# Loading the first two token tiles of x on two DMA queues and starting the first key products between their transposes

## The chip, the cores and the metric

The kernel runs on one core of a Trainium2 chip. The metric is device time in microseconds (us). The kernel before takes 179.36 us, the median of five runs (178.54 to 179.41).

## The reference

Two blocks read the same input x (2048 tokens, 512 features, bf16) and are mixed by a gate per token:

```python
x = A_x
g = _sigmoid((x * gate_w).sum(-1, keepdims=True))
a = _A_ref(x, A_wqkv, A_wo)      # linear attention, 32 heads of 16
b = _B_ref(x, B_w1, B_w3, B_w2)  # silu(x w1) * (x w3), times w2; F = 1376
return g * a + (1 - g) * b
```

In the attention block q, k, v = x wqkv; q and k go through phi(t) = (t + 1 if t > 0 else exp(t)) + 1e-6. Per head, kv is the sum over tokens of phi(k) times v and z the sum of phi(k); the output is phi(q) kv / (phi(q) z + 1e-6), times wo.

## The kernel before, in words

Tokens are cut into 16 tiles of 128, and these into four blocks of 512. All of x and all weights are held in SBUF. x is needed in two layouts: `x_sb` (tokens on partitions) and `xT` (features on partitions, in four chunks `kc` of 128). For tiles 2 to 15, `xT` comes by transposing DMAs from HBM (L87, L91). For tiles 0 and 1 TensorE makes it from `x_sb` (`emit_xT`, L169): four transposes of 128x128 against the identity `ident` per tile. They go into PSUM in two pairs; VectorE copies the pair of chunks 0 and 1 to `xT` (L179), ScalarE the pair of chunks 2 and 3 (L181).

The order of the loads is that of their issue. On the sync queue (SP): x tiles 0 and 1 in one transfer of 256 KB (L82), the second half of wk (chunks 2 and 3, L84), the transposing load of tiles 2 and 3 (L87), then the later blocks of x and the other weights. On ScalarE's queue: the first half of wk (chunks 0 and 1, L83). In the transfer of L82, partition p takes the token rows 2p and 2p + 1, which lie together in HBM (2 KB per partition); tile j then holds every second row, and the output of tiles 0 and 1 is stored back by the same view (`out_first`, L81 and L376). GpSimd (POOL) makes the identity first (L59), and then fills the block mask, the padding of w2r and two buffers `hr` (L117 to L135).

TensorE's order is the order of the code, written out by hand from L150 on. It begins with `emit_warm` (L158): matmuls on constants whose result nobody reads, six of 512 columns and three of 128 (L165). After these come the transposes of tile 0, those of tile 1, and then the key products of the first block, four per tile (one for each chunk), each of 128x512 (`emit_k_mm`, L183). The first six of them are interleaved between tiles 0 and 1:

```python
    emit_xT(0)
    emit_xT(1)
    for kc, t in ((0, 0), (1, 0), (0, 1), (1, 1), (2, 0), (3, 0)):
        emit_k_mm(k0[t], t, kc)
```

A tile's products end in `emit_k_phi` (L189): ScalarE takes exp, VectorE forms phi(k) into `pk_sb`, POOL adds it up in `pks`. From tile 4 on, products of keys alternate with those of XP, the sum over tokens of x times phi(k) (`emit_xp`, L202), from which kv is made later (L436). Then queries, the feed-forward block (`emit_ffn`, L302) and the outputs (`emit_out`, L335) follow block by block on TensorE.

Of the kernel before, what the change touches and what calls it, by code (L numbers as in the profile page):

```python
# [13 lines left out]
BF16 = mybir.dt.bfloat16  # L14
# [3 lines left out]
def kernel(  # L18
# [12 lines left out]
    nc = tc.nc  # L31
    P = nc.NUM_PARTITIONS
# [7 lines left out]
    TB = 512  # L40
# [8 lines left out]
    x2d = A_x.flatten_outer_dims()  # L49
    out2d = out.flatten_outer_dims()  # L50

    consts = ctx.enter_context(tc.tile_pool(name="consts", bufs=1))
# [2 lines left out]
    psM = ctx.enter_context(tc.tile_pool(name="psM", bufs=4, space=bass.MemoryType.PSUM))  # L55


    ident = consts.tile([P, P], BF16, name="ident")
    make_identity(nc, ident[:])  # L59


    x_sb = consts.tile([P, NT, D], BF16, name="x_sb")
    xT = consts.tile([P, KC, S], BF16, name="xT")
    wk_sb = consts.tile([P, KC, D], BF16, name="wk_sb")
# [12 lines left out]
    x_r = x2d.rearrange("(t p) d -> p t d", p=P)  # L77
    dq = nc.sync
    TF = 2
    x_first = x2d[0 : TF * P, :].rearrange("(p j) d -> p j d", j=TF)  # L80
    out_first = out2d[0 : TF * P, :].rearrange("(p j) d -> j p d", j=TF)  # L81
    dq.dma_start(out=x_sb[:, 0:TF, :], in_=x_first)  # L82
    nc.scalar.dma_start(out=wk_sb[:, 0:2, :], in_=wqkv_r[:, 0:2, D : 2 * D])  # L83
    dq.dma_start(out=wk_sb[:, 2:4, :], in_=wqkv_r[:, 2:4, D : 2 * D])  # L84
    pre = consts.tile([1, 1], FP32, name="pre")
    nc.scalar.activation(out=pre[:], in_=nc.const_aps.tensor(0.0, [1, 1], FP32), func=ACT.Exp)
    dq.dma_start(  # L87
        out=xT[:, :, TF * P : TB], in_=x2d[TF * P : TB, :], transpose=True
    )
    for tb in range(1, NTB):  # L90
        dq.dma_start(  # L91
            out=xT[:, :, tb * TB : (tb + 1) * TB], in_=x2d[tb * TB : (tb + 1) * TB, :],
# [7 lines left out]
    with nc.allow_non_contiguous_dma(reason="one gate weight per partition and chunk"):  # L100
        dq.dma_start(
            out=wr_sb[:, :, 2 * FR : NR], in_=gate_w.rearrange("(kc d o) -> d kc o", d=P, o=1)
        )
    dq.dma_start(out=wv_sb[:], in_=wqkv_r[:, :, 2 * D : 3 * D])
    for fsl in (slice(0, FM // 2), slice(FM // 2, FM)):
# [13 lines left out]
        out=bm, in_=bm, pattern=[[-Dh, HPC], [0, Dh]], compare_op=ALU.is_ge, fill=0.0,  # L119
# [3 lines left out]
        out=bm, in_=bm, pattern=[[Dh, HPC], [0, Dh]], compare_op=ALU.is_ge, fill=0.0,  # L123
# [34 lines left out]
    def emit_warm(*widths):  # L158
        warm = psX.tile([P, TB], FP32, tag="XP3", name="warm")
        for n in widths:  # L160
            nc.tensor.matmul(  # L161
                warm[:, 0:n], lhsT=warm_l, rhs=warm_r[:, 0:n], start=True, stop=True
            )

    emit_warm(TB, TB, TB, TB, TB, TB, P, P, P)  # L165

    st = {}

    def emit_xT(t):  # L169
        for h in range(2):  # L170
            xTp = psX.tile([P, 2, P], BF16, tag=f"XP{(2 * t + h) % 4}", name="xTp")
            for j in range(2):
                kc = 2 * h + j
                nc.tensor.transpose(  # L174
                    out=xTp[:, j, :], in_=x_sb[:, t, kc * P : (kc + 1) * P], identity=ident[:]
                )
            xT_t = xT[:, 2 * h : 2 * h + 2, t * P : (t + 1) * P]
            if h == 0:
                nc.vector.tensor_copy(out=xT_t, in_=xTp[:])  # L179
            else:  # L180
                nc.scalar.activation(out=xT_t, in_=xTp[:], func=ACT.Copy)  # L181

    def emit_k_mm(k_ps, t, kc):  # L183
        nc.tensor.matmul(  # L184
            k_ps[:], lhsT=xT[:, kc, t * P : (t + 1) * P], rhs=wk_sb[:, kc, :],
            start=(kc == 0), stop=(kc == KC - 1),
        )
# [148 lines left out]
    def emit_out(tb, tt):  # L336
        t = tb * TPB + tt
        tsl = slice(tt * P, (tt + 1) * P)

        if t < NT - 1:  # L340
            parts = [(0, D, True)]
        else:
            h, q7 = D // 2, 7 * D // 8
            parts = [(0, h, True), (h, q7, True), (q7, D, True)]
        if t < NT - 1:
            o_out = work.tile([P, D], BF16, tag="o_out", name="o_out")
        else:
            o_out = consts.tile([P, D], BF16, name="o_last")
        lo = 0
        for i, (a, b, store) in enumerate(parts):  # L350
            o_ps = psX.tile([P, b - a], FP32, tag=f"XP{2 + (tt + i) % 2}", name="o_ps")
            for c in range(KC):
                nc.tensor.matmul(  # L353
                    o_ps[:], lhsT=st[tb, "pqT"][:, c, tsl], rhs=W_sb[:, c, a:b],
                    start=(c == 0), stop=False,
                )
            nc.tensor.matmul(  # L357
                o_ps[:], lhsT=st[tb, "hTr"][:, tsl], rhs=w2r_sb[:, a:b],
                start=False, stop=False,
            )  # L360
            for fc in range(FC):
                nc.tensor.matmul(  # L362
                    o_ps[:], lhsT=st[tb, "hT"][:, fc, tsl], rhs=w2_sb[:, fc, a:b],
                    start=False, stop=(fc == FC - 1),
                )
            if i < 2:
                nc.scalar.activation(  # L367
                    out=o_out[:, a:b], in_=o_ps[:], func=ACT.Copy, scale=omg[:, t : t + 1]
                )
            else:  # L370
                nc.vector.tensor_scalar(  # L371
                    out=o_out[:, a:b], in0=o_ps[:], scalar1=omg[:, t : t + 1], scalar2=None,
                    op0=ALU.mult,
                )
            if store:
                rows = out_first[t] if t < TF else out2d[t * P : (t + 1) * P, :]  # L376
                eng = nc.scalar if i == 1 else nc.sync
                eng.dma_start(out=rows[:, lo:b], in_=o_out[:, lo:b])
                lo = b


    k0 = [psM.tile([P, D], FP32, tag="mm", name=f"k0_{t}") for t in range(TPB)]
    emit_xT(0)
    emit_xT(1)
    for kc, t in ((0, 0), (1, 0), (0, 1), (1, 1), (2, 0), (3, 0)):
        emit_k_mm(k0[t], t, kc)
    emit_k_phi(k0[0], 0)
    for t in range(1, TPB):
# [15 lines left out]
    with tc.manual_schedule(engines={ENG.DVE}):  # L404
# [18 lines left out]
        for dc in range(KC):  # L423
# [9 lines left out]
            out=z_sb[:].rearrange("p (b f) -> p b f", f=Q),  # L433
            in_=z_col[:, :, None].to_broadcast([P, NB, Q]),
        )
        kvT_ps = psX.tile([P, KC, P], FP32, tag="XP0", name="kvT_ps")  # L436
        for c in range(KC):
# [7 lines left out]
            out=kvT_sb[:], in0=kvT_ps[:],  # L445
# [22 lines left out]
    for tb in range(NTB):  # L468
        for fc in range(FC if tb == 0 else 0, FC):
            emit_ffn(tb, fc)  # L470
        nx = tb + 1
        for tt in range(TPB):
            if nx < NTB:
                emit_q(nx, tt, psX, "XP0")
                if tt % 2 == 0:
                    emit_rem(nx, tt // 2, psX, "XP1")
                    if tt == 2:
                        emit_omg(nx)
            emit_out(tb, tt)
            if nx < NTB:  # L480
                emit_den(nx, tt)
        if nx < NTB:
            emit_norm(nx)
# [30 lines left out]
```

## Time and profile before

| what | value |
|---|---|
| median of 5 runs | 179.36 us (178.54 to 179.41) |
| the five runs | 179.40, 179.33, 178.54, 179.41, 179.36 us |
| profiled execution's own time | 179.52 us |
| its span | 177.7 us |
| TensorE busy | 173.3 us, 98% of the span |
| VectorE busy | 118.7 us, 67% |
| ScalarE busy | 65.5 us, 37% |
| POOL busy | 63.7 us, 36% |
| HBM read, written | 8.42 MB, 2.10 MB |

All times in the profile count from the start of its span. PE is TensorE's matmuls, PEld its weight loads, DVE is VectorE, ACT ScalarE, POOL GpSimd and SP SyncE; "SPq" and "ACTq" are their DMA issues. A row of the timeline has the start, the time covered, engine, line, operation, output and inputs, and the count. A matmul's duration contains the time in the array's pipeline, so that the distance between the starts of two matmuls that follow each other is its cost, not its duration. A row of the windows has the window, its length, the busy time of PE, PEld, DVE, ACT and POOL (with counts), the granted TensorE clock, the mean busy share of the DMA engines, and GB/s. A row of the DMA issues has the line's tile and source, the queue, the count, the size, and the time from issue to landing.

### The profile page before, as it was taken

How to read it: one execution, taken by the hardware profiler on the slowest of the kernel's cores; microseconds unless marked ns; L12 is line 12 of the kernel's file. 1: busy time of each engine (PE TensorE's matmuls, PEld its weight loads, DVE VectorE, ACT ScalarE, POOL GpSimd, SP SyncE). 2: the span in 40 equal slices, each digit the busy share in tenths (PEclk: the TensorE clock that was granted, in tenths of full speed). 3: DMA queues.
4: the chain of work that ended last, by engine and by line, in shares of the span. 5: the costliest groups of instructions: out<-in, count | busy, mean ns of one | idle time of the engine just before them, and what ended most of it. 6: DMA issues, size and time to landing. Idle time of an engine off the chain costs nothing.

```text
span 177.7 us, 2457 instructions
## 1 busy us (share of the span) xinstructions
PE 173.3 (98%) x867; PEld 84.1 (47%) x883; DVE 118.7 (67%) x204; ACT 65.5 (37%) x123; POOL 63.7 (36%) x80
## 2 busy tenths in 40 slices
PE   8999999999999999999999999999999999999993
PEld 3444444474444545444454544444545444444463
DVE  0397767899999737498786375978754669776000
ACT  3543323475542434343333333242433323331222
POOL 6087755689153323262003232620032328000000
DMA  5999999921004011123000111240001022200002
GB/s 168 240 275 230 305 293 365 350 87 29 10 6 112 0 44 33 44 59 89 0 0 11 37 37 37 59 90 6 0 7 60 14 62 67 59 0 0 30 30 63
DMA packets 30380, 15.14 MB, mean 85 GB/s; under 512 B 20928, under 2 KB 30240, under 8 KB 30368
## 3 DMA queue, kind: packets, MB, share of 16 engines
q1 hardware_dynamic: 29952, 14.67, 30.2%
q10 hardware_dynamic: 416, 0.31, 0.6%
q8 instruction: 7, 0.11, 0.3%
q14 instruction: 5, 0.04, 0.1%
HBM read 8.42 MB, written 2.10 MB: 59 GB/s over the span
## 4 chain that ended last, share of the span: by engine, by line
PE 98%; issue 1%; DVE 0%
PE o_ps L362 19%; PE up_ps L320 19%; PE gate_ps L312 19%; PE o_ps L353 8%; PE XP L204 8%; PE q_ps L217 8%; PE k_ps L184 6%; PE r_ps L241 3%; PE k L184 2%; PE o_ps L357 2%; PE warm L161 2%; PE xTp L174 1%; PE kvT_ps L440 1%; PE W_ps L458 0%; DVE o_last L371 0%
## 5 line engine op out<-in xcount | busy, mean ns | idle before, releaser
L320 PE MATMUL up_ps<-xT,w_sb 128*128 128x512 bf16 x157 | 40.7, 379 | 0.2
L312 PE MATMUL gate_ps<-xT,w_sb 128*128 128x512 bf16 x157 | 40.7, 379 | 0.2
L225 POOL TENSOR_TENSOR qz<-pq,z_sb 128x512 f32<-128x512 bf16 x16 | 18.5, 1162 | 58.0 <-DVE pq L145 58.0
L325 ACT ACTIVATE th<-gate_ps 128x512 bf16<-128x512 f32 x40 | 23.9, 597 | 39.0 <-PE gate_ps L312 36.4
L362 PE MATMUL o_ps<-w_sb,hT 128*128 128x512 bf16 (+3 forms) x177 | 37.3, 355 | 0.2
L327 DVE SCALAR_TENSOR_TENSOR gs<-th,gate_ps 128x512 bf16<-128x512 bf16 x40 | 27.2, 681 | 5.4 <-ACT th L325 5.1
L332 DVE TENSOR_TENSOR hT<-up_ps,gs 128x512 bf16<-128x512 f32 x40 | 27.6, 691 | 3.7
L142 DVE TENSOR_SCALAR phi_m<-phi_e 128x512 bf16<-128x512 bf16 x32 | 13.6, 425 | 21.5 <-ACT phi_e L140 21.3
L362 PEld LDWEIGHTS <-hT 128*128 128x128 bf16 x180 | 16.9, 98 | 17.8
L320 PEld LDWEIGHTS <-w_sb 128*128 128x128 bf16 x160 | 15.7, 98 | 18.9
L312 PEld LDWEIGHTS <-w_sb 128*128 128x128 bf16 x160 | 15.6, 98 | 18.6
L292 POOL TENSOR_TENSOR pqn<-pq,rden 128x512 bf16<-128x512 bf16 x16 | 16.5, 1055 | 15.1 <-DVE rden L285 13.1
L367 ACT ACTIVATE o_out<-o_ps,omg 128x512 bf16<-128x512 f32 x15 | 10.3, 687 | 28.9 <-PE o_ps L362 28.9
L194 POOL TENSOR_TENSOR pks<-pks,pk_sb 128x512 f32<-128x512 f32 x15 | 17.4, 1161 | 7.3 <-DVE pk_sb L145 6.7
L353 PE MATMUL o_ps<-W_sb,pqT 128*128 128x512 bf16 (+3 forms) x70 | 16.7, 355 | 0.1
L204 PE MATMUL XP<-pk_sb,x_sb 128*128 128x512 bf16 x62 | 16.2, 379 | 0.1
L228 DVE TENSOR_REDUCE den<-qz 128x32 f32<-128x512 f32 x16 | 10.9, 684 | 7.9 <-POOL qz L225 7.8
L217 PE MATMUL q_ps<-wq_sb,xT 128*128 128x512 bf16 x61 | 16.1, 379 | 0.1
L140 ACT ACTIVATE phi_e<-k_ps 128x512 bf16<-128x512 f32 x12 | 7.2, 597 | 14.4 <-PE k_ps L184 14.4
L140 ACT ACTIVATE phi_e<-q_ps 128x512 bf16<-128x512 f32 x16 | 9.6, 597 | 7.8 <-PE q_ps L217 6.7
L184 PE MATMUL k_ps<-wk_sb,xT 128*128 128x512 bf16 x48 | 12.3, 379 | 0.0
L145 DVE SCALAR_TENSOR_TENSOR pq<-q_ps,phi_m 128x512 bf16<-128x512 f32 x16 | 11.1, 691 | 0.5
(60 smaller groups left out, 120.3 us busy)
## 6 DMA issues: line engine op xcount, KB each, us to landing
w_sb<-in_B_w_dram SPq DMA_DIRECT2D x4, 640.0 KB, 7.7
out_dram<-o_out SPq DMA_DIRECT2D x15, 128.0 KB, 1.9
w_sb<-in_B_w_dram SPq DMA_DIRECT2D x1, 1280.0 KB, 12.5
x_sb<-in_A_x_dram SPq DMA_DIRECT2D x2, 512.0 KB, 4.4
x_sb<-in_A_x_dram SPq DMA_DIRECT2D x1, 768.0 KB, 5.1
wq_sb<-in_A_wqkv_dram SPq DMA_DIRECT2D x1, 512.0 KB, 5.1
wv_sb<-in_A_wqkv_dram SPq DMA_DIRECT2D x1, 512.0 KB, 6.6
wo_sb<-in_A_wo_dram SPq DMA_DIRECT2D x1, 512.0 KB, 10.1
```

Source lines behind the costliest of these rows:

```text
L184: nc.tensor.matmul(k_ps[:], lhsT=xT[:, kc, t * P : (t + 1) * P], rhs=wk_sb[:, kc, :], start=(kc == 0), stop=(kc == KC - 1),)
L194: nc.gpsimd.tensor_add(pks[:], pks[:], pk_sb[:, t, :])
L204: nc.tensor.matmul(XP_ps[dc][:], lhsT=x_sb[:, t, dc * P : (dc + 1) * P], rhs=pk_sb[:, t, :], start=(t == 0), stop=(t == NT - 1),)
L217: nc.tensor.matmul(q_ps[:], lhsT=xT[:, kc, ts_tok], rhs=wq_sb[:, kc, :], start=(kc == 0), stop=(kc == KC - 1),)
L225: nc.gpsimd.tensor_tensor(out=qz[:], in0=st[tb, "pq"][:, tt, :], in1=z_sb[:], op=ALU.mult)
L312: nc.tensor.matmul(gate_ps[:], lhsT=w1_sb[:, kc, fsl], rhs=xT[:, kc, tok_sl], start=(kc == 0), stop=(kc == KC - 1),)
L320: nc.tensor.matmul(up_ps[:], lhsT=w3_sb[:, kc, fsl], rhs=xT[:, kc, tok_sl], start=(kc == 0), stop=(kc == KC - 1),)
L325: nc.scalar.activation(out=th[:], in_=gate_ps[:], func=ACT.Tanh, scale=0.5)
L327: nc.vector.scalar_tensor_tensor(out=gs[:], in0=th[:], scalar=1.0, in1=gate_ps[:], op0=ALU.add, op1=ALU.mult)
L332: nc.vector.tensor_tensor(out=st[tb, "hT"][:, fc, :], in0=up_ps[:], in1=gs[:], op=ALU.mult)
L353: nc.tensor.matmul(o_ps[:], lhsT=st[tb, "pqT"][:, c, tsl], rhs=W_sb[:, c, a:b], start=(c == 0), stop=False,)
L362: nc.tensor.matmul(o_ps[:], lhsT=st[tb, "hT"][:, fc, tsl], rhs=w2_sb[:, fc, a:b], start=False, stop=(fc == FC - 1),)
```

## The change

The identity is made after the first loads are issued. The transfer of x tiles 0 and 1 becomes two of 128 KB: tile 0 first on the sync queue, tile 1 on GpSimd's (software) queue. The tiles are now contiguous rows of x and of the output, as all others are. The loads of wk's halves keep their queues and places. One of the wide dummy matmuls goes. Tile 0's products of chunks 0 and 1 come between the transposes of tile 0 and those of tile 1.

```diff
-    ident = consts.tile([P, P], BF16, name="ident")
-    make_identity(nc, ident[:])
...
-    x_first = x2d[0 : TF * P, :].rearrange("(p j) d -> p j d", j=TF)
-    out_first = out2d[0 : TF * P, :].rearrange("(p j) d -> j p d", j=TF)
-    dq.dma_start(out=x_sb[:, 0:TF, :], in_=x_first)
+    dq.dma_start(out=x_sb[:, 0, :], in_=x_r[:, 0, :])
     nc.scalar.dma_start(out=wk_sb[:, 0:2, :], in_=wqkv_r[:, 0:2, D : 2 * D])
+    nc.gpsimd.dma_start(out=x_sb[:, 1, :], in_=x_r[:, 1, :])
+    ident = consts.tile([P, P], BF16, name="ident")
+    make_identity(nc, ident[:])
     dq.dma_start(out=wk_sb[:, 2:4, :], in_=wqkv_r[:, 2:4, D : 2 * D])
...
-    emit_warm(TB, TB, TB, TB, TB, TB, P, P, P)
+    emit_warm(TB, TB, TB, TB, TB, P, P, P)
...
-                rows = out_first[t] if t < TF else out2d[t * P : (t + 1) * P, :]
+                rows = out2d[t * P : (t + 1) * P, :]
...
     emit_xT(0)
+    emit_k_mm(k0[0], 0, 0)
+    emit_k_mm(k0[0], 0, 1)
     emit_xT(1)
-    for kc, t in ((0, 0), (1, 0), (0, 1), (1, 1), (2, 0), (3, 0)):
+    for kc, t in ((0, 1), (1, 1), (2, 0), (3, 0)):
         emit_k_mm(k0[t], t, kc)
```

## The prediction

> **What bounds the kernel now.** I read the page's busy shares and its chain of work first. Then came the chain in time order, the timeline of the first 14 us, the issues to landing, and the DMA rate in steps of 0.2 us.
>
> ```profile
> PE 173.3 (98%) x867; PEld 84.1 (47%) x883; DVE 118.7 (67%) x204; ACT 65.5 (37%) x123; POOL 63.7 (36%) x80
> PE 98%; issue 1%; DVE 0%
> ```
>
> TensorE is the chain almost alone, and the waits list shows it waiting for one transfer only (0.2 us for x). So every microsecond that the head of its queue loses or wins reaches the end, unless something later stands still anyway, and nothing does. The chain, in order of time:
>
> ```profile
> 0.84 3.04 PE warm L161 x9
> 3.88 0.97 PE xTp L174 x8
> 4.85 4.09 PE k L184 x16
> 8.95 0.86 PE XP L204 x4
> ```
>
> The head is dummy matmuls, eight transposes (both tiles), sixteen key products, then XP. How fast a product goes, from the timeline in short windows (start, duration, count):
>
> ```profile
> 3.82 0.29 PE L174 MATMUL xTp<-ident,x_sb 128*128 128x128 bf16 x1
> 4.65 0.63 PE L184 MATMUL k<-wk_sb,xT 128*128 128x512 bf16 x1
> 5.93 0.65 PE L184 MATMUL k<-wk_sb,xT 128*128 128x512 bf16 x2
> 6.19 0.60 PE L184 MATMUL k<-wk_sb,xT 128*128 128x512 bf16 x2
> 8.78 0.38 PE L204 MATMUL XP<-pk_sb,x_sb 128*128 128x512 bf16 x1
> ```
>
> Products start at 4.65, 5.07, 5.50 and 5.93 (0.427 apart), then at 6.19, and from there every 0.2155 us: 6.19 + 12 x 0.2155 = 8.78. So TensorE runs at half speed until about 6.02 and at full speed after it, though the column of the granted clock says 1.00 throughout; it does not show this gate. It opened once, after 5.18 us of nearly unbroken work. Whatever delays the opening costs half the delay.
>
> When the operands arrive (issue row, KB, us from issue to landing), and the DMA rate (last column, GB/s):
>
> ```profile
> wk_sb<-in_A_wqkv_dram ACTq DMA_DIRECT2D x1, 256.0 KB, 3.7
> x_sb<-in_A_x_dram SPq DMA_DIRECT2D x1, 256.0 KB, 3.0
> wk_sb<-in_A_wqkv_dram SPq DMA_DIRECT2D x1, 256.0 KB, 4.0
> ...
> 2.20:2.40 0.20, 0.20 (x2) 0.03 (x1) 0.00 (x0) 0.20 (x1) 0.15 (x1) 1.00 0.10 41
> 2.40:2.60 0.20, 0.20 (x2) 0.09 (x1) 0.00 (x0) 0.19 (x2) 0.18 (x1) 1.00 0.86 338
> ```
>
> Issued at 0.81 and 0.80, x lands at 3.81 and wk's first half at 4.50; the second half lands at 5.27. Both streams begin at about 2.4 and then share some 340 GB/s. Today x lands just as the dummies run out, wk's first half 0.15 us before its first use, and VectorE's copy of xT is ready just as the eighth transpose has issued. The head has no bubble to remove.
>
> **The change, part by part.**
>
> *Dummy matmuls.* One of six wide ones goes: minus 0.427 us. They now end their issue at 0.84 + 5 x 0.427 + 3 x 0.107 = 3.30.
>
> *x tile 0 alone on sync.* 128 KB in 1 KB packets beside wk's 1 KB packets, where 2 KB packets stood before. [...] It lands at about 3.4 (3.2 to 3.6), 0.4 sooner. The number of issues on SP and ACT is the same, so wk's second half (1.27) and the transposing loads behind it keep their issue times; the second half is first used after 6.4, and the loads for tiles 2 and 3 land at 1.73 + 4.5 = 6.2, used after 7.3.
>
> *wk's first half,* which the first products need. [...] it moves no fewer bytes ahead of wk, and now three queues share. [...] landing 4.15 to 4.50; I take 4.35. If only tile 0 counted, products could start at 3.45 + 0.80 = 4.25; wk makes it **4.40**.
>
> *x tile 1 by gpsimd.* No row shows such a DMA. Nearest rows: a 128 KB store lands in 1.9 us, x in 3.0 us. Below, 1.9 us; above, 4.5 us (the slow transposing load's). [...] I take 3.4: landing at 4.2, range 2.7 to 5.3. It is needed when the two early products have issued: 4.40 + 0.85 = 5.25. Hidden, with about 1 us to spare; without that cover each microsecond late costs one.
>
> *The identity moves behind that DMA on POOL,* as do the blockmask, w2r and hr fills. The identity was ready at 1.47 and first used at 3.82. Now it is needed at 3.45, [...]. The fills end at 3.69 before, and POOL then waits 4.8 us for pk: cost nothing.
>
> *The output rows of tiles 0 and 1* go out contiguous instead of every second row: same bytes and pieces, far from the end: nothing.
>
> *The new order on TensorE.* From the first transpose of a tile to its first product takes 3.82 to 4.62, 0.80 us (transpose, VectorE copy 0.29, weight load). Before, all eight transposes (8 x 0.107 = 0.86) covered it. Now four cover 0.43 of it, twice. Tile 0: transposes 3.45 to 3.88, then idle to 4.40 (copy and wk). Products of tile 0: 4.40 to 5.25. Transposes of tile 1: 5.25 to 5.68, then idle until its copy: third product at 5.25 + 0.80 = **6.05**. Queued behind that wait are the fourteen products left and everything after them. If the gate opens at 6.02 as before, XP starts at 6.05 + 14 x 0.2155 = 9.07 against 8.78: **+0.29 us**. With wk at its early end the copy sets 4.25 and it would be +0.20; at wk's late end +0.45.
>
> *The gate.* New idle: 0.15 + 0.52 + 0.37 = 1.0 us between 3.30 and 6.05. [...] I take it that it fails, narrowly. By the row alone (same opening): +0.29. [...] The new order then has done 2 + 3.38/0.427 = 9.9 products by 9.43, the old one 19: 9.1 x 0.2155 = **+1.96 us**.
>
> Against the profiled execution, 179.52 us (span 177.7, 1.8 around it, which I leave alone), that is 181.48. The median is 0.16 lower; I carry the difference over: 179.36 + 1.96 = **181.3 us**.
>
> **Rivals.**
> - *The gate opens on time.* [...] Then 179.36 + 0.29 = 179.65, not measurably slower. [...] A variant: the opening slips by the idle alone, to about 7.04; then 4.3 products are done against 7.9: +0.78, 180.1.
> - *Faster.* Place: wk's arrival and the opening. One run of five took 178.54, 0.82 below the others; at half speed that is an opening 1.64 us earlier, 4.38. With it, and wk landed by 4.25: products at 4.25, then everything at full speed, third product at 5.45, XP at 8.47: -0.31, 179.05. With x 0.3 us earlier still, it passes 0.54. It needs both; a landing of wk after about 4.6 undoes it.
> - *The software queue is late,* or the gate wants 5.18 unbroken us again. If tile 1 lands at 6.8, the third product is at 7.6: +1.55 with the gate on time. With opening at 6.05 + 5.18 = 11.23: 14.1 products against 27.4, +2.87, 182.2.
> - *The change does nothing,* as TensorE is full anyway: excluded unless idle stays under the removed 0.43 us; the sum of copies alone is 2 x 0.37.
>
> **How the numbers follow.** [...] 181.3: 0.43. Opens on time, 179.65: 0.30. Slips by the idle, 180.1: 0.10. Late queue or long gate, 181 to 182.2: 0.10. Earlier opening, 179.05 or less: 0.07. Range 179.4 to 182.0; its low end is the on-time case with wk early, its high end takes in most of the late cases. A change under 0.3% (0.54 us) cannot be told from none here. Faster by more than that 0.05, within 0.32, slower 0.63. The likeliest case alone: 181.0 to 181.6.
>
> **What would show it.** Transposes in two groups of four; the first near 3.45; wk's first half at 4.15 to 4.5; a bubble near 0.5 us before the first product and 0.37 before tile 1's; products 0.427 apart until about 9.4. Products 0.2155 apart from 6.05 would prove the gate step wrong and leave +0.3. A wait for x tile 1 past 5.3, or a wait for the identity, would put the cost on POOL's queue instead.

## The result, and the profile after

The changed kernel takes 179.70 us, the median of 38 runs (179.40 to 182.22); the kernel before, over 73 runs, 179.14 us (178.53 to 179.84). The ratio is 1.006, with a 95% interval of 1.0045 to 1.0076: slower by 0.6%, where 1.1% was forecast. The ratio leaves out the two slowest of the 38 runs.

The median hides the form. 27 runs lie between 179.40 and 180.11 (median 179.56), 11 between 181.49 and 182.22 (median 181.73), none between. I call these the common and the late group. By means over all runs: 180.27 against 179.08, +1.19 us. The common group's mean is 179.63, so the common group is +0.56 above before, and the rest, 11/38 x (181.82 - 179.63) = 0.63, comes from the late group.

The profiled execution (180.11 us, span 178.4) is of the common group. Its chain, in order of time (start, us, what):

```profile
1.31 4.50 DMA x_sb<-in_A_x_dram
5.81 0.05 issue
5.85 0.30 PE xTp L171 x2
6.15 0.02 issue
6.18 0.30 DVE xT L176
6.48 0.05 issue
6.53 3.20 PE k L181 x14
```

Before, the chain began with the dummies on TensorE. Now a transfer leads it: x tile 1, issued by GpSimd at 1.31 and landed at 5.81. Behind it stand two transposes, a copy, and fourteen key products. TensorE's waits for data in the first 14 us, before (first row) and after (who, for what: us in total, times, longest):

```profile
PEld L174 <- DMA x_sb<-in_A_x_dram: 0.2, 1, 0.2
...
PEld L171 <- DMA x_sb<-in_A_x_dram: 1.7, 1, 1.7
PE xTp L171 <- DMA x_sb<-in_A_x_dram: 0.8, 1, 0.8
PE k L181 <- DVE xT L176: 0.3, 1, 0.3
PE k L181 <- DMA wk_sb<-in_A_wqkv_dram: 0.2, 1, 0.2
```

The weight load and the matmul of one transpose wait side by side, so the first two rows of after are one wait and do not add. The DMA issues that answer to those of before:

```profile
wk_sb<-in_A_wqkv_dram ACTq DMA_DIRECT2D x1, 256.0 KB, 3.2
wk_sb<-in_A_wqkv_dram SPq DMA_DIRECT2D x1, 256.0 KB, 3.5
...
x_sb<-in_A_x_dram SPq DMA_DIRECT2D x1, 128.0 KB, 2.3
x_sb<-in_A_x_dram POOLq DMA_DIRECT2D x1, 128.0 KB, 4.5
```

Tile 0 came at 0.81 + 2.3 = 3.1, wk's first half at 4.0 instead of 4.5. But tile 1 took 4.5 us. Products, from the timeline in short windows:

```profile
4.07 0.60 PE L181 MATMUL k<-wk_sb,xT 128*128 128x512 bf16 x1 [0.18 <-DMA wk_sb<-in_A_wqkv_dram]
4.46 0.63 PE L181 MATMUL k<-wk_sb,xT 128*128 128x512 bf16 x1
5.85 0.23 PE L171 MATMUL xTp<-ident,x_sb 128*128 128x128 bf16 x1 [0.76 <-DMA x_sb<-in_A_x_dram]
6.53 0.39 PE L181 MATMUL k<-wk_sb,xT 128*128 128x512 bf16 x1 [0.28 <-DVE xT L176]
6.75 0.59 PE L181 MATMUL k<-wk_sb,xT 128*128 128x512 bf16 x2
9.56 0.38 PE L201 MATMUL XP<-pk_sb,x_sb 128*128 128x512 bf16 x1
```

From the third product on they are 0.2155 us apart: here the fast spacing had come in time. XP starts at 9.56 against 8.78. That start is a yardstick: in the profiles of before, after and all those below, the execution's time minus XP's start is 170.5 to 170.9 us. So to within 0.4 us, all that differs is decided ahead of XP.

### The profile page after: what moved, and what is told of

The parts are those of the page before. It is cut to its first block, busy times and chain, and to the rows that moved or that the text cites. A ratio compares the mean times of both kernels' runs of the same rounds, so it can differ in the third digit from the quotient of the medians.

```text
span 178.4 us, 2457 instructions
## 1 busy us (share of the span) xinstructions
PE 172.8 (97%) x866; PEld 83.5 (47%) x882; DVE 118.6 (66%) x204; ACT 65.5 (37%) x123; POOL 64.5 (36%) x81
## 4 chain that ended last, share of the span: by engine, by line
PE 95%; DMA 3%; issue 1%; DVE 0%; POOLq 0%
PE o_ps L359 19%; PE up_ps L317 19%; PE gate_ps L309 19%; PE o_ps L350 8%; PE XP L201 8%; PE q_ps L214 8%; PE k_ps L181 6%; PE r_ps L238 3%; DMA x_sb<-in_A_x_dram 3%; PE o_ps L354 2%; PE k L181 2%; PE kvT_ps L439 1%; PE W_ps L457 0%; DVE xT L176 0%; PE xTp L171 0%
```

## The experiments

"Late" means 181 us or more; none of the runs of before reached it. The opening is the moment at which the spacing of the products changes from 0.427 to 0.2155 us, worked out as in the prediction. What the recorded texts call gate or clock is this change; the column of the granted clock reads 1.00 on both sides of it in the profiles of before and after, so the traces show the two spacings and not what sets them.

**Tile 1 on the sync queue (E1).** The rest as changed:

```diff
     dq.dma_start(out=x_sb[:, 0, :], in_=x_r[:, 0, :])
+    dq.dma_start(out=x_sb[:, 1, :], in_=x_r[:, 1, :])
-    nc.gpsimd.dma_start(out=x_sb[:, 1, :], in_=x_r[:, 1, :])
```

> The changed kernel with x tile 1 back on the sync queue, right behind tile 0; the rest as changed. Theory (tile 1 lands late because it goes by GpSimd's queue): it lands at about 4.2 instead of 5.81, TensorE waits for no x before tile 1's transposes, the third key product starts near 5.9 instead of 6.53, XP near 9.0 instead of 9.56; +0.2 us on before where the clock opens on time. Rival (the new order itself is the cost, whatever the queue): third product still near 6.5, XP near 9.5.

Measured: ratio 1.0038 (1.0017 to 1.0058). The common group (19 of 22) has a median of 179.38, and 3 runs are late. From the chain of its profile:

```profile
4.10 0.59 PE k L181 x2
4.70 0.13 PE xTp L171 x2
4.82 0.02 issue
4.84 0.30 DVE xT L176
5.15 0.04 issue
5.19 3.20 PE k L181 x14
```

Tile 1 was issued at 1.26 and landed at 4.44, and TensorE no longer waits for it; the copy alone (0.30 and what lies around it) stands between. XP starts at 8.23, but the opening came before 4.1 in this profile, so its earliness is not the queue's alone. Between the common groups the queue is worth 179.56 - 179.38 = 0.2 us, or 0.1 against the repeat below (179.47). The late group does not need GpSimd's queue: 3 of these 22 runs are late without it.

**The order alone (E2).** The kernel before, its loads and six wide dummies, with the two early products moved ahead of tile 1's transposes:

```diff
     emit_xT(0)
+    emit_k_mm(k0[0], 0, 0)
+    emit_k_mm(k0[0], 0, 1)
     emit_xT(1)
-    for kc, t in ((0, 0), (1, 0), (0, 1), (1, 1), (2, 0), (3, 0)):
+    for kc, t in ((0, 1), (1, 1), (2, 0), (3, 0)):
```

> The kernel before with TensorE's new order alone (same loads, six wide dummies). Theory: x lands at 3.8, the first product starts at 4.6, tile 1's transposes near 5.5, third product near 6.3, XP near 9.3: +0.4 to +0.5 us on before where the clock opens near 6. Rival (order costs nothing, only the late tile 1 does): XP at 8.8 to 8.9, no change.

Measured: ratio 1.0029 (1.0016 to 1.0041), none of 22 runs late, mean +0.50 us (179.53 against 179.03). Its timeline:

```profile
4.52 0.60 PE L184 MATMUL k<-wk_sb,xT 128*128 128x512 bf16 x2 [0.27 <-DVE xT L179]
4.96 0.39 PE L174 MATMUL xTp<-ident,x_sb 128*128 128x128 bf16 x4
5.62 3.19 PE L184 MATMUL k<-wk_sb,xT 128*128 128x512 bf16 x14 [0.28 <-DVE xT L179]
```

There is a wait of 0.27 to 0.28 us for VectorE's copy before either group of products. This is the order's price with no software queue in play, and it is nearly as large (0.50) as what the whole change costs in its common group (0.56). XP starts at 8.66 in this profile, ahead of the 8.78 of before, because its opening came before 4.5; the price is read from the 22 runs.

**The loads alone (E3), and the same with the idle filled (E12).** E3 has the changed loads and five wide dummies, with the old order. E12 adds four dummies where TensorE stands (against E3):

```diff
     emit_xT(0)
+    emit_warm(TB, TB, TB, TB)
     emit_xT(1)
     for kc, t in ((0, 0), (1, 0), (0, 1), (1, 1), (2, 0), (3, 0)):
```

> The changed kernel's loads and five wide dummies, TensorE's order as before (all eight transposes first). Theory of the late tile 1: products begin only after 5.85 plus some 0.3, all sixteen at full speed if the clock is open then, XP near 9.6: +0.8 us. [...] TensorE stands for some 2.1 us before 5.85, so nearly all runs show the late opening, +2 us or more. Rival (the 2 us of some runs have to do with the order of the products): no runs 2 us late here.

> The kernel with the changed loads and the old order (13 of its 21 runs were about 2 us late), with four wide dummies between tile 0's transposes and tile 1's, where TensorE stood for 1.5 us or more. [...] the late group is gone and the runs lie at 179.4 to 180.2. Rival (late groups come from the transfer): about 6 in 10 stay above 181.

Measured: E3 1.0101 (1.0073 to 1.0128), 13 of 21 runs late, where one theory expected nearly all and the rival none. E12 1.0037 (1.0021 to 1.0053), 0 of 16 late, all between 179.35 and 180.54. The waits for x in E3's profile, then in E12's:

```profile
PEld L171 <- DMA x_sb<-in_A_x_dram: 1.5, 1, 1.5
PE xTp L171 <- DMA x_sb<-in_A_x_dram: 1.3, 1, 1.3
```

```profile
PEld L171 <- DMA x_sb<-in_A_x_dram: 0.8, 2, 0.4
```

The dummies compute nothing that is read, and tile 1 still lands at 5.1 and 5.4 in the two profiles. What they change is that TensorE does not stand before tile 1, and the late group is gone. A late transfer as its cause is out.

**The changed kernel with the idle filled (E4).** Two wide dummies between the early products and tile 1's transposes:

```diff
     emit_k_mm(k0[0], 0, 1)
+    emit_warm(TB, TB)
     emit_xT(1)
```

> The changed kernel with two more wide dummy matmuls between tile 0's two early products and tile 1's transposes; they run while TensorE waits for tile 1 anyway. [...] the group of runs 2 us late (11 of 38 of the changed kernel) is gone, the others stay at 179.4 to 180.1. Rival (the late group comes from the transfer or from the launch, not from idle time on TensorE): about 3 in 10 runs stay near 181.7.

Measured: ratio 1.0042 (1.0021 to 1.0062), 0 of 10 late. At 11 late in 38, ten runs without one would come by chance about once in thirty times, so E12 is the stronger proof. The middle is 180.00, not 179.56, and 3 of the 10 lie above the 180.1 expected. The likely reason: where the spacing is still 0.427 us, two dummies take 0.85 us and end at 4.89 + 0.85 = 5.7, after tile 1 has landed (5.0 here). That is an estimate; in the profiled run, one of the two fastest (179.37), the opening came at about 4.5 and they took 0.43. The dummies trade the late group for a later common one.

**Fewer dummies in the kernel before (E5).** Nothing on the path moves; x lands at 3.81 whatever TensorE does until then:

```diff
-    emit_warm(TB, TB, TB, TB, TB, TB, P, P, P)
+    emit_warm(TB, TB, TB, P, P, P)
```

> The kernel before with three wide dummies fewer (three wide, three narrow), nothing else: TensorE stands from about 2.4 until x lands at 3.81, and nothing that it computes afterwards waits for longer. [...] slower than before by 0.4 to 0.8 us in the middle of the runs, with single runs up to 180.5 or later. Rival (only waits on the path count, idle before the operands land is free): no change, all runs within 178.5 to 179.8.

Measured: ratio 1.0088 (1.0063 to 1.0113) over six runs, 179.58 to 180.84, mean +1.5 us; more than expected. Its chain:

```profile
0.81 3.02 DMA x_sb<-in_A_x_dram
...
3.88 1.03 PE xTp L174 x8
4.91 4.49 PE k L184 x16
```

Transposes and products start when they did before (3.88 and 4.91 against 3.88 and 4.85), but the sixteen products take 4.49 us instead of 4.09: the opening came at about 6.9. This is the 179.83 run, still within the spread of before. The other runs are 179.58 and four between 180.64 and 180.84, slower than every run of before; they have no profile, but by the yardstick XP starts near 10.1 in them, which puts the opening at about 8.6 (an estimate). Between the two kernels only idle time that nobody waits for differs, so it costs time; in the profiled run it does so by the later opening (6.9 instead of 6.02).

**Both halves of wk on ScalarE's queue (E6).** The kernel before with

```diff
     nc.scalar.dma_start(out=wk_sb[:, 0:2, :], in_=wqkv_r[:, 0:2, D : 2 * D])
-    dq.dma_start(out=wk_sb[:, 2:4, :], in_=wqkv_r[:, 2:4, D : 2 * D])
+    nc.scalar.dma_start(out=wk_sb[:, 2:4, :], in_=wqkv_r[:, 2:4, D : 2 * D])
```

> The kernel before with wk's second half on ScalarE's queue behind its first half, so that the second half no longer shares the DMA engines with the first. Theory [...]: the first half lands at 4.1 to 4.3 instead of 4.50; products start up to 0.2 us sooner where the clock is open early, not sooner where it opens near 6 (eight transposes at half speed end at 4.65): 0 to -0.2 us. Rival (second half now too late, its first use is near 5.4 with an early clock): 0 to +0.5 us, with a wait for wk before the fifth product.

Measured: 1.0012 (0.9999 to 1.0025). The first half still lands 3.7 us after its issue; the expected 4.1 to 4.3 failed. But the edit did not leave it without company: on the sync queue the transposing load of tiles 2 and 3 moved up into the place of wk's second half (in before, the second issue of that queue is at 1.27, the third at 1.73). So the run does not decide what the second half's company costs the first.

**GpSimd's queue in a quiet place (E7, E9).** E9 makes the tile depend on late data:

```diff
                 emit_den(nx, tt)
+                if nx >= 2 and tt == 0:
+                    spare = consts.tile([P, D], BF16, name=f"spare{nx}")
+                    nc.gpsimd.tensor_copy(spare[:], st[nx, "pq"][:, 0, :])
+                    (nc.gpsimd if nx == 2 else nc.sync).dma_start(out=spare[:], in_=x_r[:, 1, :])
```

> The kernel before with two spare loads of x tile 1 (128 KB) that nobody reads, where the queues are nearly empty: one by GpSimd in the third token block, one by sync in the fourth. Theory (the software queue itself is slow): the sync load lands in about 2.0 us, GpSimd's in 3.5 or more. Rival (the 3.7 to 4.5 us of the head come from sharing the DMA engines there): both land in about 2.0 to 2.5 us.

> The kernel before with two spare 128 KB loads of x tile 1, each into a tile that GpSimd has just written from late data, so that they start near 90 us (GpSimd's queue) and near 130 us (sync), where the DMA engines are nearly empty. Theory (the software queue's own start is the cost): sync's lands in about 2.0 us, GpSimd's in 3.0 or more. Rival (sharing the engines at the head is the cost): both in 2.0 to 2.5 us.

E7 did not reach a quiet place: without the copy, the two loads were scheduled at 3.6 and 31.9, amid other loads, and landed after 6.0 (GpSimd) and 7.0 us (sync). In E9 they were issued at 97.1 (GpSimd) and 133.7 (sync):

```profile
spare<-in_A_x_dram POOLq DMA_DIRECT2D x1, 128.0 KB, 2.5
spare<-in_A_x_dram SPq DMA_DIRECT2D x1, 128.0 KB, 2.2
```

Alone, the software queue is 0.3 us slower. At the head it took 3.7 to 4.5 us, so 1.2 to 2.0 us come with the other loads there, as the rival of these two expectations had it. The queue is not free of blame, though: in nearly the same company the sync queue took 3.2 us for the same tile (E1). Which queue the transfer stands on, and its place among the others, is worth 0.5 to 1.3 us there. E1 also issues wk's second half 0.46 us later, so the two are not told apart.

**Plain loads beside tile 1 (E8).** The changed kernel with wq's load moved ahead of the transposing loads:

```diff
     dq.dma_start(out=wk_sb[:, 2:4, :], in_=wqkv_r[:, 2:4, D : 2 * D])
+    dq.dma_start(out=wq_sb[:], in_=wqkv_r[:, :, 0:D])
```

> The changed kernel with the load of wq (512 KB, plain) moved on the sync queue ahead of the transposing loads, so that GpSimd's transfer of x tile 1 shares the engines with plain loads alone. What is read is x tile 1's landing; the time itself suffers from the late tiles 2 and 3. Theory A [...]: it lands in 3.0 us or less from its issue at 1.31. Theory B (the software queue's own start is the cost): still 3.7 or more.

Tile 1 still took 3.7 us, so it is not the transposing loads in particular that hold it up. What three queues cost one another at the head stays open. The run took 181.97 us, and its profile shows the late opening a first time, beside a wait for tiles 2 and 3:

```profile
7.97 0.63 PE L181 MATMUL k<-wk_sb,xT 128*128 128x512 bf16 x1
9.20 0.61 PE L181 MATMUL k<-wk_sb,xT 128*128 128x512 bf16 x1 [0.59 <-DMA xT<-in_A_x_dram]
...
9.91 0.60 PE L181 MATMUL k<-wk_sb,xT 128*128 128x512 bf16 x2
```

From the third product (5.86) to the wait they stand about 0.427 us apart; only from 9.91 on are they 0.2155 apart. The opening came at about 9.8.

**The version meant as better (E10).** Tile 1 on sync as in E1, both halves of wk on ScalarE's queue as in E6, and

```diff
-    for kc, t in ((0, 1), (1, 1), (2, 0), (3, 0)):
+    for kc, t in ((2, 0), (3, 0), (0, 1), (1, 1)):
```

> Meant as the better version: x tile 0 and tile 1 one behind the other on sync, both halves of wk on ScalarE's queue, and tile 0's other two products put between tile 1's transposes and tile 1's first product, so that they cover its copy. If the copy's bubble and the late tile 1 are the cost of the changed kernel's common runs: no idle before tile 1's first product, XP at 7.8 with an early clock and 8.7 with a late one: -0.1 to -0.3 us on before. If wk's second half lands later than 5 us: a wait for wk there, and no gain.

Measured: 1.0023 (1.0009 to 1.0036), none of 22 late, slower than before. The bubble of tile 1's copy is covered, and TensorE does not wait for wk in the profiled run (179.89), whose opening came only at about 6.8: the transposes issue until 5.31 and tile 0's third product follows at once. But wk's second half lands at about 5.25. In a run with an early opening the products would have to wait for it: XP at 5.25 + 14 x 0.2155 = 8.27 at best, against about 7.8 in the fastest runs of before, an estimate of 0.5 us. No such run was profiled; the fastest run, 179.21, is 0.7 us above the fastest of before. No version here beats the kernel before.

**The changed kernel again (E11, and three single runs), and E3 once more.**

> The changed kernel again, for more runs beside the others: two groups as before, about 7 in 10 at 179.4 to 180.1 and 3 in 10 near 181.7. In the profile, GpSimd's transfer lands 3.7 to 4.5 us after its issue at 1.31; in a run of the late group the products would stand 0.427 us apart until beyond 8.

> The changed kernel, one look, in the hope of a run of the late group (about 2 in 10). [...] in a run above 181.4 the key products stand 0.427 us apart until 9 or later; in a run below 180.2 they are 0.2155 apart from the third product on. Rival (late transfer): in a late run some transfer lands 2 us later than else, and products are 0.2155 apart around it.

> The changed kernel, a second look, with the same expectation as for the first.

> The changed kernel, a third look, with the same expectation as for the first.

> The changed loads with the old order, one look; 13 of its 21 runs were late. [...] in a run above 181 the sixteen key products stand 0.427 us apart until about 9; else they are 0.2155 apart. Rival (late transfer): products 0.2155 apart after a transfer that lands 2 us later than the 5.12 seen before.

E11: 1.0036 (1.002 to 1.0052); 20 of 22 runs common (median 179.47), 2 late. Its profile (179.46 us) had the fast spacing by 4.06, tile 1 landed at 5.16:

```profile
4.06 0.39 PE L181 MATMUL k<-wk_sb,xT 128*128 128x512 bf16 x1 [0.17 <-DVE xT L176]
4.28 0.38 PE L181 MATMUL k<-wk_sb,xT 128*128 128x512 bf16 x1
5.21 0.28 PE L171 MATMUL xTp<-ident,x_sb 128*128 128x128 bf16 x2 [0.55 <-DMA x_sb<-in_A_x_dram]
5.88 0.39 PE L181 MATMUL k<-wk_sb,xT 128*128 128x512 bf16 x1 [0.28 <-DVE xT L176]
```

The second and third single runs took 179.69 and 179.77 (third product at 6.10 and 6.09), that of E3's kernel 179.54, so no late run of E3's kernel was profiled. The first took 181.45: a run of the late group, in profile. Its products:

```profile
6.28 0.61 PE L181 MATMUL k<-wk_sb,xT 128*128 128x512 bf16 x1 [0.17 <-DVE xT L176]
6.68 0.63 PE L181 MATMUL k<-wk_sb,xT 128*128 128x512 bf16 x1
...
7.53 1.06 PE L181 MATMUL k<-wk_sb,xT 128*128 128x512 bf16 x2
...
8.81 0.74 PE L181 MATMUL k<-wk_sb,xT 128*128 128x512 bf16 x2
9.17 0.59 PE L181 MATMUL k<-wk_sb,xT 128*128 128x512 bf16 x2
...
10.68 0.38 PE L201 MATMUL XP<-pk_sb,x_sb 128*128 128x512 bf16 x1
```

The third product starts at 6.28, earlier than in the first profile (6.53). Seven products then stand about 0.427 us apart, and the spacing falls to 0.22 only from 9.17 on. No transfer is late: tile 1 landed at 5.4, as in the second and third single runs. The late group is the late opening, here at about 9.1.

## Why the prediction was wrong, step by step

The effects were there and the sign was right; the size was not. Forecast for the median were +1.94 us; between the medians of 38 and 73 runs it is +0.56, between the means +1.19. One step was taken as certain that holds in some runs only.

- **The gate: the step that failed.** "I take it that it fails, narrowly", with an opening at 9.43. Nothing in the profile of before showed an opening that late. In a late run it is so: the opening comes at 9.1 there, and the late group (181.73) lies near the 181.3 predicted. But it is late in 11 of 38 runs, and in 2 of 22 of the repeat, not in all. The sum charged the late opening, 1.96 - 0.29 = 1.67 us, to every run; the runs paid 2.19 us in 11 of 38, which is 0.63 in the mean and 0.14 in the median (179.70 against the common group's 179.56). The error behind it is the fixed opening at 6.02. Four of the five times shown lay within 0.08 us, and I read one fixed opening out of that. The 73 runs of before spread over 1.3 us; if the opening alone makes that spread, it moves by 2.6 us from run to run (an estimate: by the spacings of 0.427 and 0.2155 us, half of a delay is lost). The profiles show it. With the head of before unchanged, the opening came at 6.0 (before, E9) and 6.6 (E7); in the changed kernel before 4.1 (E11), between 4.7 and 5.2 (second single run) and at 9.1 (first). An opening that moves so far makes some runs late and others not.
- **What the opening depends on.** That the work left would fall just short was an assumption; no trace shows that an amount decides it, nor what moves the opening from run to run. TensorE's work up to 3.25 us is the same in all five profiles of the changed kernel, and the opening still came before 4.1 in E11 and at 9.1 in the first single run, in which TensorE had stood for 0.41 + 0.38 + 0.23 us between 3.25 and 5.5. Over many runs idle time does tell: three dummies fewer cost 1.5 us in the mean (E5), and with the idle filled 0 of 16 runs are late instead of 13 of 21 (E12).
- **x tile 1 "hidden, with about 1 us to spare".** Wrong: in the five profiles of the changed kernel it lands at 5.81, 5.16, 5.4, 5.4 and 5.4, not at 4.2. In the first of them the early products had issued by 4.9 (4.46 + 0.43), since wk came sooner than I took. Two terms were mis-sized. The 4.2 counts from an issue at 0.8, but GpSimd issued at 1.31, which is 0.5 of the delay. And the latency was 3.8 to 4.5 us, not 3.4, an estimate for a queue of which before has no row. The queue alone is worth 0.3 (E9); the rest comes with the other loads, amid which even the sync queue took 3.2 us for this tile (E1).
- **wk at 4.35, first product at 4.40.** 4.0 and 4.07 in the first profile, 4.2 and 4.35 in the second single run. Tile 0 at 3.4: between 3.1 and 3.6. Both were my estimates; no trace of before shows how transfers on several queues share their time. These gains were real and bought nothing, as the third product waits for tile 1 and its copy.
- **The new order: +0.29 us with the opening on time.** The place was right: a wait of 0.28 us for the copy in the profile. E2 gives +0.50 for the order alone. With an early opening, the old order gains more from it: the kernel before has runs at 178.5, E2 none under 179.07. The sum at one opening could not see that.
- **The on-time rival, 179.65.** The common group's median is 179.56: near, but in part by luck: an early wk and a late tile 1 stand in place of the numbers I gave.
- **The identity and fills on POOL** cost nothing, as taken: POOL's issue took 0.70 us, the identity was ready at 2.7, and in the first profile the first transpose went at 3.25 without a wait.

## What to carry to other kernels

Where the head of a kernel runs while TensorE's products still stand 0.427 us apart instead of 0.2155, idle time there had two prices here: the wait itself, and the chance that the opening comes some 4 us later (at 9.1 instead of 4.7 to 5.2 in two runs of one kernel). A few runs that agree do not show when the opening comes; take the spread of many, and the products' spacing in more than one profile. When work is brought forward on an engine that takes it in the code's order (in E3, TensorE stood 1.28 us for tile 1, until 5.17, with tile 0's products behind that wait and wk's first half landed at 4.0), count what used to cover the latency that now stands bare: here, before, tile 1's four transposes (0.43 us) covered the copy of tile 0 (0.30) at no cost.

## What was not expected of the hardware

- Three dummy matmuls that nobody waits for are worth 0.9% of this kernel (E5, six runs). The granted-clock column read 1.00 in the profiles with the late and with the early opening.
- The same 128 KB by GpSimd took 2.5 us on quiet queues (E9), and 3.7 to 4.5 at the head beside loads of which two were issued 0.5 us earlier. Its issue began at 1.31 us, where GpSimd's first fill had begun at 0.80 before.
